# Decode step of two attention and two GLU layers: keeping one more V tile and passing the layer change through five single slots

## The chip, the cores and the metric

The kernel runs on one core of a Trainium2 chip. The metric is device time in microseconds of one execution, taken as the median of several executions. A core has a matrix engine (PE, with its weight loads shown apart as PEld), a vector engine (DVE), a scalar engine (ACT), a general engine (POOL) and a sync engine (SP). In this kernel SP issues all the large transfers from HBM into the on-chip memory (SBUF), in one fixed order; they run on 16 DMA engines that the core has. Sums of matrix products stand in PSUM, a memory of eight banks.

## What is computed

A residual block of attention and a residual block of a gated GLU, run twice with the same weights, for four sequences with one new token each:

```python
def _A_ref(x, k_cache, v_cache, wq, wo):        # x: 4 x 1 x 512
    W = min(4096, max(256, Sk // 4))            # 2048 of 8192 cached positions
    rep = Hq // Hkv                             # 32 query heads, 8 K/V heads
    q = (x @ wq)...                             # 4 x 32 x 1 x 128
    k = jnp.repeat(k_cache[:, :, Sk - W:, :], rep, axis=1)
    v = jnp.repeat(v_cache[:, :, Sk - W:, :], rep, axis=1)
    p = _softmax(q @ k.T * (Dh ** -0.5))
    return (p @ v)... @ wo

def _B_ref(x, w_gate, w_up, w_down):            # 512 -> 1792 -> 512
    return (_sigmoid(x @ w_gate) * (x @ w_up)) @ w_down

x = x + _A_ref(_layernorm(x), ...)
x = x + _B_ref(_layernorm(x), ...)
x = x + _A_ref(_layernorm(x), ...)
x = x + _B_ref(_layernorm(x), ...)
```

All weights and caches are bf16. The part of K that is read is 16 MB, that of V 16 MB, `wq` and `wo` are 4 MB each, the three GLU weights 1.8 MB each. Both attentions read the same caches and weights.

## The kernel before

**Memory.** One SBUF array, `arena`, is cut into 50 slots of 512 KB (128 partitions of 4096 bytes). Two neighbouring slots are a tile of 1 MB. Slots 0 to 31 hold all of K, loaded once and kept for both attentions. The other 18 slots are nine tiles of a pool (`pool`, line 372). Through these pass the V tiles (two per head, named `("V", h, bp, k)` with k = 0 or 1 for the first or second layer), `wq`, `wo` and the GLU weights. The four tiles of `wo` (two heads each) are loaded once in the first layer and kept to the end.

**Order of the loads.** A list `loads` (lines 1393 to 1420) fixes the order in which SP issues transfers. `fill` takes from its head as long as a place is free; the work that reads a place ends with `done`, which frees it. On the chip this becomes a wait of SP for the engine that last read the slot, and SP takes its queue strictly in order. In the first layer each head h brings K of head h + 2, every even head one tile of `wo` (`load_wo`), and then its two V tiles. After the last V come the GLU weights (`load_glu(0)`), `wq` for the second layer (`load_wq(1)`), the V tiles of the second layer from head 7 down, and the second GLU.

**What is kept over the layer change.** V of head 7 stays: tile Y = (7, 0) is moved into PSUM banks by four DVE transposes (`stash`, lines 564 to 570) and moved back later (`load_stash`, lines 572 to 581), so that its two slots are free meanwhile; tile Z = (7, 1) stays where it is, but its first half is also put into PSUM (`stash_half`, `unstash_half`), so that its first slot is free. V tile (6, 1) stays as a whole (`stay`, line 1396). The other 13 V tiles are read again.

**What passes through the change.** `homes` gives a load a fixed slot in place of one from the pool. Before the change there are seven such single slots: both of Y, the first of Z, and both of the tiles GA and GB, which first held the gate weights `wg` in two loads of 896 KB. Then follow, slot by slot, four loads of `wu`, four of `wd`, the second half of `wq` in four loads of 512 KB (`q_mms(1, 1, ...)` reads them), the first half of `wq` in two loads of 1 MB, and V tiles (6, 0) and (5, 1) in halves, in GA and GB.

**Order of the work.** In the first layer and the first GLU a planner (`_schedule`, line 92) picks the order on each engine from estimated durations and landing times; from `q_second` on (`P.chain`, line 1429) PE keeps the order of the program. `attn_first` (line 1146) runs, per head, four DVE transposes of K (line 830), scores (lines 848 and 859), a softmax (lines 872 to 887), a turn of the probabilities (lines 900 to 907), the product with V (`pv_unit`, line 949) and the product with `wo` (`wo_unit`, line 1137). `glu` (line 1268) runs eight groups of matmuls on `wg` and `wu` (line 1309) and four on `wd` (line 1377; in the last layer three, line 1352). `attn_second` (line 1167) begins with scores of head 7, between whose mask and products stand the first two groups of the first half of q (`q_mms(1, 0, OBS[1], (0, 1))`, line 1201; its matmuls are on line 769). Its V products for the first seven heads are `pv_wide` (line 1033); they use scratch in the place of a `wq` tile (`wide_buffers`, line 981). Only the last head goes through `pv_unit` and `wo_unit` again.

Of the kernel before, what the change touches and what calls it, by code (L numbers as in the profile page):

```python
# [278 lines left out]
def build(nc, A_x, A_k, A_v, A_wq, A_wo, B_wg, B_wu, B_wd, out, cfg=None):  # L279
# [42 lines left out]
    with es:  # L322
# [97 lines left out]
        GA = ("wg", 0, 0)  # L420
        GB = ("wg", 1, 0)
# [11 lines left out]
        def take_load():  # L433
            take_k()
            assert can_take()
            name, emit = loads.pop(0)
            if name in homes:
                hfree.difference_update(home(name))
                s = home(name)[0]
            else:  # L440
                s = pool.alloc()
            where[name] = s
            if name in (Y, Z, GA, GB):
                base[name] = s
            emit(s)
# [73 lines left out]
        def load_wq(k):  # L519
            if k == 0:  # L520
                for c in range(NC):
                    load(("wq", c, k), 2, "bw_8k", (2 * SLOT, wq_d[:, c, :], False))
            else:
                for c in range(NC):
                    load_half(("wq", c, k), wq_d[:, c, SLOT:2 * SLOT], "bw_4k", SLOT, ((Y, 1), (Z, 0), (GA, 0), (GA, 1))[c])
                for cc in range(NC // 2):
                    name = ("wq", (0, cc), k)
                    load(name, 2, "bw_4k", (2 * SLOT, wq_d[:, 2 * cc:2 * cc + 2, 0:SLOT], False))
                    homes[name] = [((GB, Y)[cc], 0), ((GB, Y)[cc], 1)]
                    if cc == 0:  # L530
                        on_free[name] = lambda s: hfree.add(s + 1)

        def wq_part(k, c, i):

            if k == 0:
                return ("wq", c, k), i * SLOT
            if i == 1:
                return ("wq", c, k), 0
            return ("wq", (i, c // 2), k), (c % 2) * SLOT

        def load_wo(hh):
            load(("wo", hh), 4, "bw_4k", (2 * SLOT, wo_d[:, hh * 2:(hh + 1) * 2, :], False))

        def load_glu(k):
            for nm, src in (("wg", wg_d), ("wu", wu_d)):
                if k == 0 and nm == "wu":
                    for c in range(NC):
                        load_half((nm, c, k), src[:, c, :], "bw_3k", F, ((Y, 0), (Y, 1), (Z, 0), (GA, 0))[c])
                    continue
                for cc in range(NC // 2):  # L550
                    load((nm, cc, k), 2, "bw_3k", (2 * F, src[:, 2 * cc:2 * cc + 2, :], False))
            on_free[GA] = lambda s: hfree.add(s + 1)
            on_free[GB] = lambda s: hfree.add(s + 1)
            for (a, b) in bounds_of(k):
                if k == 0:
                    load_half(("wd", a, k), wd_d[:, a:b, :].rearrange("p k n -> p (k n)"), "bw_4k", (b - a) * D,
                              ((GA, 1), (GB, 0), (GB, 1), (Y, 0))[a // 4])
                else:
                    load(("wd", a, k), 1, "bw_8k", ((b - a) * D, wd_d[:, a:b, :], False))
# [34 lines left out]
        def load_v(h, bp, k, n_use):  # L594
            name = ("V", h, bp, k)
            tile = {(HKV - 2, 0): GA, (HKV - 3, 1): GB}.get((h, bp)) if k else None
            if tile is not None:
                for n in range(2):
                    load_half((name, ("Vh", h, bp, k))[n], pair_d(A_v, h, bp)[:, :, n * SLOT:(n + 1) * SLOT], "bw_4k", SLOT, (tile, n))
                del on_free[name]  # L600
                halves[name] = ("Vh", h, bp, k)
                return
            load(name, n_use, "bw_8k", (2 * SLOT, pair_d(A_v, h, bp), True))
# [153 lines left out]
        def q_mms(k, i, qb, cs, keep_last=False):  # L757
            for c in cs:
                name, o = wq_part(k, c, i)
                s = need(name)  # L760

                half = k == 1 and i == 1
                src = slot_ap(s) if half else tile_ap(s)
                rd = tok(s) if k == 0 else tok(s)[:1] if half else tok(s)[c % 2:c % 2 + 1]

                def e_q(pe, c=c, src=src, o=o):
                    last = None
                    for hh in range(4):
                        last = pe.matmul(ps[32 * hh:32 * hh + NB, qb, :], xn[:, c * NB:(c + 1) * NB],  # L769
                                         src[:, o + hh * 512:o + (hh + 1) * 512],  # L770
                                         start=(c == 0), stop=(c == NC - 1))
                    return last
                P.op("tensor", "q%d_%d_%d" % (k, i, c), 4 * tm["pe_row"], e_q,
                     r=rd + [("xn",)], w=[("qrow", i)], banks=(qb,))
                if not (keep_last and c == NC - 1):
                    done(name)
                if k == 1 and i == 0 and c == 0:
                    give(s)
# [22 lines left out]
        def q_second(variance):  # L801
            q_mms(1, 1, WB, (0, 1))
            variance()
            unstash_half(())
            q_mms(1, 1, WB, (2, 3))
            fresh.append(q_turn(1, 1, WB))
# [174 lines left out]
        def wide_buffers(s, op):  # L981
            f = tile_ap(s).bitcast(F32)
            n = 0
            for name, size in (("tv", 512), ("o32", 32), ("osh", 32), ("rm", 64), ("rv", 8), ("pr", 8)):
                for k2 in range(2):
                    rest[name, k2] = f[:, n:n + size]
                    if name == "tv":
                        rest["dg", k2] = f[:, n:n + 544]
                    n += size
            for k2 in range(2):  # L990
                rest["A", k2] = f[:, n:n + 128].bitcast(BF16)
                n += 128
            rest["op"] = op
            rest["mb"] = f[:, n:n + 64]
            P.op("gpsimd", "mb", 200.0,
                 lambda g: g.tensor_copy(rest["mb"].rearrange("p (b x) -> p b x", b=2),
                                         maskb.unsqueeze(2).broadcast_to([128, 2, 32])),
                 r=[("maskb",)], w=[("mb",)], after=(op,))

        def sums(tag, k2):  # L1000
# [7 lines left out]
                 lambda pe: pe.matmul(out_, rest["mb"], pr, start=True, stop=True),  # L1008
                 r=[("pr", k2), ("mb",)], w=[("psb", k2)], banks=(sbank,))
# [8 lines left out]
        def pv_wide(tag, h, k2, tiles):  # L1018
            ob = OBS[k2]
            ew = ebuf[:, k2 * 256:(k2 + 1) * 256].bitcast(BF16).rearrange("p (g n x t) -> p g n t x", g=4, n=2, t=2)  # L1020
            ss = dict((bp, need(name)) for bp, name in tiles)
            for bp, name in tiles:
                if name in halves:
                    need(halves[name])

            def e_pv(pe):
                last = None
                for n in range(4):
                    mq, t = n // 2, n % 2
                    for g in range(4):  # L1030
                        jh, bp = g // 2, g % 2
                        src = tile_ap(ss[bp])[:, (jh * 16 + 8 * mq) * 128:(jh * 16 + 8 * mq + 8) * 128]
                        last = pe.matmul(ps[32 * g:32 * g + 32, ob, :], ew[:, g, mq, t],  # L1033
                                         src.rearrange("p (m t d) -> p t m d", t=2, d=128)[:, t], start=(n == 0), stop=(n == 3))
                return last
            P.op("tensor", "PV" + tag, 16 * tm["pe_row"], e_pv,
                 r=tok(ss[0]) + tok(ss[1]) + [("e", k2)], w=[("pso", k2, 0), ("pso", k2, 1)], banks=(ob,))
            for bp, name in tiles:
                done(name)
# [38 lines left out]
        def wo_wide(tag, h, op, k2, first, final):  # L1078
# [4 lines left out]
            def e_wo(pe):  # L1083
                last = None
                for m in range(REP):
# [4 lines left out]
                 r=tok(s) + [("opb", k2)], w=[("psr",)], banks=(PBS[1],))  # L1090
            done(name)

        def wo_compact(tag, h, op, k2):
# [4 lines left out]
            def e_wo(pe):  # L1098
                last = None
                for m in range(REP):  # L1100
# [6 lines left out]
                 r=tok(s) + [("opb", k2)], w=[("psw",)], banks=(WB,))  # L1107
# [20 lines left out]
        def wo_unit(tag, h, ov, k2, first, final):  # L1128
# [4 lines left out]
            def e_wo(pe):  # L1133
                last = None
                for r_ in range(REP):
# [7 lines left out]
                 r=tok(s) + [("op", k2)], w=[("psw",)], banks=(WB,))  # L1143
# [23 lines left out]
        def attn_second():  # L1167
# [33 lines left out]
            score(0, lambda: q_mms(1, 0, OBS[1], (0, 1)))  # L1201
# [4 lines left out]
            s = need(wq_part(1, NC - 1, 0)[0])  # L1206
            left[wq_part(1, NC - 1, 0)[0]] += 1
            q_mms(1, 0, OBS[1], (2, 3))
            wide_buffers(s, P.ops[-1])
# [58 lines left out]
        def glu(k, b0, b1, last=False):  # L1268
# [31 lines left out]
            for n, nm in enumerate(("wg", "wu")):  # L1300
                for c in range(NC):
                    piece = k == 0 and n == 1
                    name = (nm, c if piece else c // 2, k)
                    s = need(name) + (0 if piece else c % 2)
# [10 lines left out]
                    if k == 0 and n == 0 and c % 2 == 0:  # L1315
                        give(s)
# [79 lines left out]
        stay = keep[1:] + [(HKV - 2, 1)]  # L1396
# [3 lines left out]
        for h in range(HKV):  # L1400
            if h + 2 < HKV:
                loads.append((("K", h + 2), lambda _, h=h + 2: load_k(h)))
            if h % 2 == 0:
                load_wo(h // 2)
            for bp in range(2):
                load_v(h, bp, 0, 2 if (h, bp) in keep + stay else 1)
        load_glu(0)
# [3 lines left out]
        for h in range(HKV)[::-1]:  # L1411
            v_tiles[(0, h)] = [(bp, ("V", h, bp, 0)) for bp in range(2)]
            v_tiles[(2, h)] = [(bp, ("V", h, bp, 0 if (h, bp) in stay else 1)) for bp in range(2)[::-1]]
            for bp in range(2)[::-1]:
                if (h, bp) not in keep + stay:
                    load_v(h, bp, 1, 1)
                    n_v += 1
                    if n_v == cfg.get("ST", 2):
# [84 lines left out]
```

## Time and profile before

| What | Value |
|---|---|
| median of 3 runs | 180.72 us (180.55 to 181.25) |
| profiled execution, span | 178.8 us |
| busy: PE, DVE, ACT, POOL | 101.7, 104.4, 32.7, 21.5 us |
| bytes read from HBM | 70.78 MB |
| DMA, 20 to 80 us | 418 to 419 GB/s |
| DMA, 104 to 128 us (the layer change) | 358 to 417 GB/s in pieces of 4 us |
| first V product of head 7 in the first layer | 102.2 us |
| first GLU matmul | 108.46 us |
| first matmul of q for the second layer | 119.71 us |
| first softmax step of the second layer | 129.16 us |
| last matmul | ends at 176.15 us |

The page of the profile gives, per engine, the time in which it was busy, and then the span in 40 slices with the share of busy time in tenths. A row of a timeline gives the start, the time, the engine, the line of the kernel, the operation with its destination and source, the count of merged instructions and, in brackets, the idle time of that engine just before and what ended it. The instruction by which SP issues a transfer is line 398 (`SPq`); the transfer itself lands later. The trace also keeps, for each transfer, when each of the 16 DMA engines reported its part; the last of these reports is called its landing here.

### The profile page before, as it was taken

Reading aid. Unit: us, or ns where it says so; the run is one execution under the profiler, and the core shown is the slowest. Engines: PE = TensorE matmul, PEld = TensorE weight load, DVE = VectorE, ACT = ScalarE, POOL = GpSimd, SP = SyncE. Lnnn points to the kernel's source line nnn. Section 1 sums busy time; section 2 is a strip of 40 time slices with the busy share of each in tenths; the row PEclk is TensorE's granted clock in tenths of the full one; section 3 lists DMA queues with packets and bytes.
Section 4 is the critical chain, followed back from the end, with each engine's and each line's share of the span. In section 5 each row is a group of like instructions: output and inputs, shape, how many; then the busy total and the mean of one; then the engine's idle time right before and its main releaser. Section 6 shows DMA issues by size and latency. Waiting matters only on the chain.

```text
span 178.8 us, 3879 instructions
## 1 busy us (share of the span) xinstructions
PE 101.7 (57%) x1641; PEld 55.1 (31%) x1653; DVE 104.4 (58%) x256; ACT 32.7 (18%) x87; POOL 21.5 (12%) x87
## 2 busy tenths in 40 slices
PE   0635326481933626506436857455886999766743
PEld 0202101241521412403414743231322444435311
DVE  7308997838476384593564483324199999751431
ACT  2002031221030300301102001000143455430101
POOL 6100010101010100100101000000011543351000
PEclk9999999999999999999999999999999999975555
DMA  5999999999999999999999999999999999999980
GB/s 184 418 429 427 422 423 416 414 422 420 422 413 419 420 423 422 411 421 422 423 411 420 414 401 387 407 360 421 410 395 418 423 420 422 412 418 402 410 353 22
DMA packets 12802, 71.05 MB, mean 397 GB/s; under 512 B 1256, under 2 KB 1264, under 8 KB 6640
## 3 DMA queue, kind: packets, MB, share of 16 engines
q1 hardware_dynamic: 12776, 70.79, 96.9%
q8 instruction: 13, 0.21, 0.5%
q14 instruction: 5, 0.04, 0.1%
q10 hardware_dynamic: 8, 0.00, 0.0%
HBM read 70.78 MB, written 0.00 MB: 396 GB/s over the span
## 4 chain that ended last, share of the span: by engine, by line
DMA 35%; DVE 33%; PE 19%; SPq 4%; issue 4%; ACT 2%; POOL 1%; DVEq 0%; ACTq 0%
DMA arena<-in_A_v_cache_dram 20%; DVE arena L830 11%; DMA arena<-in_B_w_down_dram 9%; PE ps L859 7%; DVE nmax L872 5%; DMA arena<-in_A_wq_dram 5%; SPq L398 4%; PE ps L949 3%; DMA arena<-in_B_w_up_dram 2%; PE ps L848 2%; DVE arena L1041 2%; DVE nmax L876 2%; DVE ebuf L907 2%; DVE mxt L880 2%; PE ps L1137 1%
## 5 line engine op out<-in xcount | busy, mean ns | idle before, releaser
L830 DVE STREAM_TRANSPOSE arena<-arena 128x1024 f32<-128x1024 f32 x32 | 37.0, 1202 | 0.0
L859 PE MATMUL ps<-arena,qbd 128*32 128x512 bf16 x256 | 25.8, 539 | 0.0
L949 PE MATMUL ps<-ebuf,arena 128*128 128x8 bf16 x576 | 17.8, 168 | 9.2 <-DMA arena<-in_A_v_cache_dram 6.1
L872 DVE TENSOR_REDUCE nmax<-ps 128x1 f32<-128x512 f32 x16 | 10.8, 676 | 19.9 <-PE ps L859 19.8
L848 PE MATMUL ps<-msk_m,msk_s 128*32 128x512 bf16 x64 | 8.6, 526 | 23.0 <-DVE arena L830 21.8
L949 PEld LDWEIGHTS ps<-ebuf,arena 128*128 128x128 bf16 x576 | 16.8, 104 | 11.3 <-DMA arena<-in_A_v_cache_dram 7.3
L887 ACT ACTIVATE prow<-ps,nmax 128x512 bf16<-128x512 f32 x16 | 11.0, 687 | 35.1 <-DVE nmax L884 29.5
L823 ACT CAST qbd<-ps 128x256 bf16<-128x256 f32 x16 | 5.9, 370 | 45.4 <-PE ps L859 35.2
L916 POOL CAST s<-psm 128x1 bf16<-128x1 f32 x9 | 1.7, 188 | 84.1 <-ACT prow L887 84.1
L859 PEld LDWEIGHTS ps<-arena,qbd 128*32 128x32 bf16 x256 | 8.4, 122 | 10.6 <-issue 7.8
L902 ACT CAST prow<-ps 128x512 bf16<-128x512 f32 x16 | 9.4, 586 | 9.9 <-PE ps L949 2.1
L769 PE MATMUL ps<-arena,xn 128*4 128x512 bf16 x64 | 8.3, 575 | 5.0 <-DMA arena<-in_A_wq_dram 4.7
L907 DVE STREAM_TRANSPOSE ebuf<-prow 128x256 f32<-128x256 f32 x16 | 7.0, 435 | 3.8 <-ACT prow L902 3.7
L848 PEld LDWEIGHTS ps<-msk_m,msk_s 128*32 128x32 bf16 x64 | 1.7, 98 | 24.0 <-DVE arena L830 22.6
L1309 PE MATMUL ps<-arena,xn 128*4 128x448 bf16 x64 | 7.2, 559 | 3.4 <-DMA arena<-in_B_w_up_dram 2.3
L818 PE MATMUL ps<-qh,eyew 32*128 32x64 bf16 x64 | 5.6, 217 | 4.8 <-ACT qbd L823 2.4
L746 ACT ACTIVATE lnv<-ps 128x4 f32<-128x4 f32 x4 | 0.7, 174 | 41.5 <-PE ps L742 41.5
L1033 PE MATMUL ps<-arena,ebuf 128*32 128x512 bf16 x112 | 7.4, 384 | 0.2 <-DVE nmax L884 0.2
L957 DVE TENSOR_TENSOR onb<-ps,rinv 128x16 bf16<-128x16 f32 x9 | 1.7, 185 | 9.7 <-PE ps L949 9.7
L784 DVE STREAM_TRANSPOSE ebuf<-ps 128x512 f32<-128x512 f32 x3 | 2.2, 717 | 8.4 <-PE ps L769 8.2
L1137 PE MATMUL ps<-onp,arena 128*128 128x16 bf16 x144 | 5.3, 175 | 2.4 <-DVE onp L972 2.4
L818 PEld LDWEIGHTS ps<-qh,eyew 32*128 32x128 bf16 x64 | 3.3, 106 | 9.8 <-ACT qbd L823 5.4
(111 smaller groups left out, 131.1 us busy)
## 6 DMA issues: line engine op xcount, KB each, us to landing
arena<-in_A_v_cache_dram SPq DMA_DIRECT2D x27, 1024.0 KB, 21.4
arena<-in_A_k_cache_dram SPq DMA_DIRECT2D x16, 1024.0 KB, 25.1
arena<-in_A_wq_dram SPq DMA_DIRECT2D x6, 1024.0 KB, 8.4
arena<-in_A_wo_dram SPq DMA_DIRECT2D x4, 1024.0 KB, 24.7
arena<-in_B_w_gate_dram SPq DMA_DIRECT2D x4, 896.0 KB, 16.3
arena<-in_B_w_down_dram SPq DMA_DIRECT2D x4, 512.0 KB, 6.4
arena<-in_A_wq_dram SPq DMA_DIRECT2D x4, 512.0 KB, 8.2
arena<-in_A_v_cache_dram SPq DMA_DIRECT2D x4, 512.0 KB, 6.8
```

The lines of the kernel that those rows point to most:

```text
L769: last = pe.matmul(ps[32 * hh:32 * hh + NB, qb, :], xn[:, c * NB:(c + 1) * NB], src[:, o + hh * 512:o + (hh + 1) * 512], start=(c == 0), s ...
L818: last = pe.matmul(dst[:, :, a * REP:(a + 1) * REP], eyew[32 * hh:32 * hh + 32, 96 - 32 * a:224 - 32 * a], src, start=True, stop=True)
L830: P.op("vector", "T%d_%d" % (h, t), c_dve(1024), lambda v, v32=v32: v.transpose(v32, v32), r=[("slot", 4 * h + t)], w=[("slot", 4 * h + t)])
L848: last = pe.matmul(ps[32 * gi:32 * gi + 32, bank, :], msk_s[:, :], msk_m[:, :].unsqueeze(1).broadcast_to([128, 256, 2]), start=True, stop= ...
L859: last = pe.matmul(ps[32 * gi:32 * gi + 32, bank, :], qbd[:, q0:q0 + 32], kt[:, cp // 2, cp % 2, jh * NJ:(jh + 1) * NJ, :], start=False, s ...
L872: lambda v: v.tensor_reduce(nmax[:, k2:k2 + 1], ps[:, bank, :], AXX, ALU.max),
L887: lambda a: a.activation(prow[:, :].rearrange("p (m x t) -> p m x t", x=32, t=2), ps[:, bank, :].rearrange("p (m t x) -> p m x t", x=32, t ...
L902: P.op("scalar", "pc" + tag, c_act(512), lambda a: a.copy(prow[:, :], ps[:, pb, :]), r=[("ppb", pb)], w=[("prow",)], banks=(pb,))
L907: P.op("vector", "pt" + tag, c_dve(256), lambda v: v.transpose(et, prow[:, :].bitcast(F32)), r=[("prow",)], w=[("e", k2)])
L949: last = pe.matmul(ps[:, ob, bp * 8:bp * 8 + 8], src[:, j * 128:(j + 1) * 128], ev[:, j % 2, j % 16 // 2, x0:x0 + 8], start=(j == 0), stop ...
L1033: last = pe.matmul(ps[32 * g:32 * g + 32, ob, :], ew[:, g, mq, t], src.rearrange("p (m t d) -> p t m d", t=2, d=128)[:, t], start=(n == 0) ...
L1309: last = pe.matmul(ps[32 * g:32 * g + NB, gub[n], 0:NF], xn[:, c * NB:(c + 1) * NB], slot_ap(s)[:, g * NF:(g + 1) * NF], start=(c == 0), s ...
```

## The change

It does four things together.

- The last tile of `wo` (heads 6 and 7) leaves its place ahead of V of head 6 and is loaded behind the last V, as two transfers of 512 KB (`wo6`, `wo7`). Readers of `wo` now wait for the slot of their head alone.
- V tile (6, 0) joins `stay`, so that 12 V tiles are read again, not 13.
- GA is gone. GB becomes an empty pair of slots that is taken from the pool behind `wo7`. The layer change passes through five single slots: both of GB, both of Y, and the first of Z. `wg`, `wu`, `wd` of the first GLU and both halves of `wq` are all loaded slot by slot (448, 448, 512 and 512 KB, the last of `wd` 256 KB). V tile (5, 1) comes in two halves, into the second slot of GB and the first of Y.
- The first group of the first half of q moves from between mask and products of head 7 to `q_second`, in front of the transposes of the second half. The scratch of `wide_buffers` lies in two single slots, with a mask of its own in each. The stash of V (7, 0) comes back behind one V tile of the second layer, not two; in both kernels that is behind (5, 1).

```diff
-        GA = ("wg", 0, 0)
-        GB = ("wg", 1, 0)
+        GB = ("pair",)
...
-            if name in (Y, Z, GA, GB):
+            if name in (Y, Z, GB):
                 base[name] = s
+            if name == GB:
+                hfree.update((s, s + 1))
             emit(s)
...
-                for c in range(NC):
-                    load_half(("wq", c, k), wq_d[:, c, SLOT:2 * SLOT], "bw_4k", SLOT, ((Y, 1), (Z, 0), (GA, 0), (GA, 1))[c])
-                for cc in range(NC // 2):
-                    name = ("wq", (0, cc), k)
-                    load(name, 2, "bw_4k", (2 * SLOT, wq_d[:, 2 * cc:2 * cc + 2, 0:SLOT], False))
...
+                for i in (1, 0):
+                    for c in range(NC):
+                        load_half(("wq", c, k, i), wq_d[:, c, i * SLOT:(i + 1) * SLOT], "bw_4k", SLOT,
+                                  (((GB, 1), (Y, 0), (Y, 1), (GB, 0)), ((Y, 0), (Z, 0), (Y, 1), (GB, 0)))[i][c])
...
         def load_wo(hh):
-            load(("wo", hh), 4, "bw_4k", (2 * SLOT, wo_d[:, hh * 2:(hh + 1) * 2, :], False))
+            left["wo", hh] = 4
+
+            def emit(s):
+                for n in range(2):
+                    dma("wo%d" % (2 * hh + n), slot_ap(s + n), wo_d[:, 2 * hh + n, :], w=[("slot", s + n)], rate="bw_4k")
+
+            if 2 * hh + 2 < HKV:
+                load(("wo", hh), 4, "bw_4k", (2 * SLOT, wo_d[:, hh * 2:(hh + 1) * 2, :], False))
+            else:
+                loads.append((("wo", hh), emit))
...
             for nm, src in (("wg", wg_d), ("wu", wu_d)):
-                if k == 0 and nm == "wu":
+                if k == 0:
                     for c in range(NC):
-                        load_half((nm, c, k), src[:, c, :], "bw_3k", F, ((Y, 0), (Y, 1), (Z, 0), (GA, 0))[c])
+                        load_half((nm, c, k), src[:, c, :], "bw_3k", F,
+                                  (((GB, 0), (GB, 1), (Y, 0), (Y, 1)), ((Z, 0), (GB, 0), (GB, 1), (Y, 0)))[nm == "wu"][c])
...
                     load_half(("wd", a, k), wd_d[:, a:b, :].rearrange("p k n -> p (k n)"), "bw_4k", (b - a) * D,
-                              ((GA, 1), (GB, 0), (GB, 1), (Y, 0))[a // 4])
+                              ((Y, 1), (Z, 0), (GB, 0), (GB, 1))[a // 4])
...
-            tile = {(HKV - 2, 0): GA, (HKV - 3, 1): GB}.get((h, bp)) if k else None
...
+            tiles = {(HKV - 3, 1): ((GB, 1), (Y, 0))}.get((h, bp)) if k else None
...
             q_mms(1, 1, WB, (2, 3))
+            q_mms(1, 0, OBS[1], (0,))
             fresh.append(q_turn(1, 1, WB))
...
-            score(0, lambda: q_mms(1, 0, OBS[1], (0, 1)))
+            score(0, lambda: q_mms(1, 0, OBS[1], (1,)))
...
-            s = need(wq_part(1, NC - 1, 0)[0])
-            left[wq_part(1, NC - 1, 0)[0]] += 1
+            slots = []
+            for c in (NC - 2, NC - 1):
+                name = wq_part(1, c, 0)[0]
+                slots.append(need(name))
+                left[name] += 1
             q_mms(1, 0, OBS[1], (2, 3))
-            wide_buffers(s, P.ops[-1])
+            wide_buffers(slots, P.ops[-1])
...
-        stay = keep[1:] + [(HKV - 2, 1)]
+        stay = keep[1:] + [(HKV - 2, 1), (HKV - 2, 0)]
...
-            if h % 2 == 0:
+            if h % 2 == 0 and h + 2 < HKV:
                 load_wo(h // 2)
             for bp in range(2):
                 load_v(h, bp, 0, 2 if (h, bp) in keep + stay else 1)
+        load_wo(HKV // 2 - 1)
+        loads.append((GB, lambda s: None))
         load_glu(0)
         load_wq(1)
...
-                    if n_v == cfg.get("ST", 2):
+                    if n_v == cfg.get("ST", 1):
                         load_stash(("V",) + keep[0] + (1,))
```

What is left out of the diff carries the same through: `pv_wide` takes its V from four slots in place of two tiles, `glu` takes each group of weights from a slot of its own, and the readers of `wo` name one slot.

## The prediction

> **What bounds the kernel now.** I read the page first, for the load on the engines and the DMA.
>
> ```profile
> PE 101.7 (57%) x1641; PEld 55.1 (31%) x1653; DVE 104.4 (58%) x256; ACT 32.7 (18%) x87; POOL 21.5 (12%) x87
> ...
> DMA  5999999999999999999999999999999999999980
> GB/s 184 418 429 427 422 423 416 414 422 420 422 413 419 420 423 422 411 421 422 423 411 420 414 401 387 407 360 421 410 395 418 423 420 422 412 418 402 410 353 22
> ...
> q1 hardware_dynamic: 12776, 70.79, 96.9%
> ```
>
> No engine is busy for much over half of the span, and the DMA engines always are, at some 420 GB/s, except in slices 24 to 30 (103 to 134 us), the layer change. So bytes set the time, as long as transfers are issued early enough. Next, therefore, the transfers of the layer change (issues in the window 92 to 135 us: count, size, median us from issue to landing) and the line of SP's issues in 90 to 135 us.
>
> ```profile
> arena<-in_A_wq_dram SPq DMA_DIRECT2D x4, 512.0 KB, 8.2
> ...
> arena<-in_A_v_cache_dram SPq DMA_DIRECT2D x4, 512.0 KB, 6.8
> ...
> arena<-in_B_w_up_dram SPq DMA_DIRECT2D x4, 448.0 KB, 5.9
> arena<-in_B_w_down_dram SPq DMA_DIRECT2D x3, 512.0 KB, 6.0
> ```
>
> ```profile
> DMA to landing us min/median/max: 4.3/7.2/10.4
> ```
>
> I call the time from issue to landing the lead. It shows how much work the DMA engines still had in front of a transfer. The shortest lead is 4.31 us (`wu` c = 3, issued at 109.04, landed at 113.35), and it landed 1.11 us behind its forerunner, the plain time of its 0.459 MB. So 4.3 us is still enough.
>
> Last, the timeline where the second attention ends (start, time, engine, line; in brackets what ended the idle time before).
>
> ```profile
> 159.92 1.01 PE L949 MATMUL ps<-ebuf,arena 128*128 128x8 bf16 x32 [0.41 <-DMA arena<-in_A_v_cache_dram]
> ...
> 161.84 0.21 PE L1067 MATMUL ps<-msks,arena 64*128 64x8 bf16 x2 [0.47 <-POOL arena L1053]
> 162.32 0.59 PE L1102 MATMUL ps<-opb,arena 128*128 128x4 bf16 x16 [0.27 <-ACT opb L1073]
> 162.77 0.99 PE L949 MATMUL ps<-ebuf,arena 128*128 128x8 bf16 x32
> ```
>
> ```profile
> 171.38 0.92 PE L1309 MATMUL ps<-arena,xn 128*4 128x448 bf16 x8 [1.30 <-DMA arena<-in_B_w_up_dram]
> ...
> 173.89 1.02 PE L1352 MATMUL ps<-arena,hT 128*4 128x128 bf16 x32 [1.17 <-DMA arena<-in_B_w_down_dram]
> 175.11 1.01 PE L1352 MATMUL ps<-arena,hT 128*4 128x128 bf16 x24 [0.20 <-DMA arena<-in_B_w_down_dram]
> ```
>
> The last V product (162.77) follows a chain of POOL, ACT and PE, not its V, which landed at 162.37. Only from 171.38 on does PE wait for weights again. So from the first softmax step (129.16) to about 170 the second attention runs at its own pace, and the DMA sets the end by the last `wu` and `wd` alone.
>
> **What goes.** One V tile is 1.049 MB; at 420 GB/s (slices 2 to 23) that is 2.5 us of DMA. It lies behind the layer change, so every landing after (5, 1) comes 2.5 us earlier if the DMA never runs dry: the last `wu` at 168.85 and not 171.34, the three `wd` at 171.35, 172.55 and 173.2 and not 173.85, 175.07 and 175.69. The bytes up to the end of `wq` are the same as before, so those landings keep their places.
>
> **What the end can take of it.** With the attention unmoved, the mean and variance end at 169.11 and PE goes through: `wu` c = 0 to 3 from 169.17 to 171.0 (two rows of 0.92), transpose 171.05 to 171.70, product 171.74 to 171.96 (0.65 and 0.22, as at 172.35 and 173.04), first `wd` at 172.10 (0.36 from the start of the product to it, as at 114.67 and 115.03), then 1.02, 0.60 and 0.41: 174.1, against 176.15 now. That is a gain of 2.05. If the attention starts at least 0.45 earlier, the `wd` landings bind again and the gain is 2.5.
>
> **The start of the second attention.** Now two groups of q (row at 126.33, 1.07 for both) stand between mask and scores of head 7; the second becomes the only one. The first goes to PE behind the group that ends at 124.34, when its 512 KB have landed (the old pair landed at 126.27, so the first half at about 125.0): 125.05 to 125.65, and the spread of q (line 818, now 125.63) follows with no loss. Scores come one group earlier, by 0.45 to 0.5. The four DVE transposes that bring Y back (0.62 each, 130.67 to 133.14) keep their place behind the first softmax.
>
> **wo behind the last V.** V of heads 6 and 7 lands one place earlier: (6, 0) 94.49, (6, 1) 96.98, (7, 0) 99.47, (7, 1) 101.95, then `wo6` 103.2, `wo7` 104.44. The V product of head 6 is bound by the turn of its softmax (98.95 to 100.8), as now. Head 7 follows at 101.4 and 102.4 in place of 102.20 and 104.48. `wo` of head 6 waits until 103.25, of head 7 until 104.6 (oe, pm, oq as now: 1.1 us behind V), against 106.39. First GLU matmul: 106.7, against 108.46. But the last `wg` lands at 108.90 as before, so GLU meets the same landings, and the 1.8 us buy only earlier issues. PE's queue behind the waiting `wo` holds nothing but head 7 and the layer norm. The stash (four of 0.68) moves from 101.97 to 99.5; it can hold up one small DVE step by 0.68, under the wait for `wo6`.
>
> **The five slots.** For each load I take the end of the last reader from the rows of its kind (0.55 us for a group of `wg` or `wu`, 0.60 for q, 0.57 for `wd`), and as landing the same place in the byte order now.
>
> | load, slot | freed by | issue | lands | lead |
> |---|---|---|---|---|
> | wg 2, 3 (Y) | V of head 7, stash | 102.5, 102.9 | 107.78, 108.90 | 5.3, 6.0 |
> | wu 0 (Z) | half stash behind oq, 0.73 | 105.3 | 110.02 | 4.7 |
> | wu 1, 2 (GB) | wg 0, 1 | 107.3, 107.85 | 111.14, 112.24 | 3.8, 4.4 |
> | wu 3, wd 0 (Y) | wg 2, 3 | 108.45, 109.55 | 113.35, 114.63 | 4.9, 5.1 |
> | wd 1 (Z) | wu 0 | 111.0 | 115.91 | 4.9 |
> | wd 2, 3 (GB) | wu 1, 2 | 111.8, 112.9 | 117.19, 117.87 | 5.4, 5.0 |
> | q2 0 (Y) | wu 3 | 114.0 | 119.10 | 5.1 |
> | q2 1 (Z) | wd 1 | 116.6 | 121.16 | 4.6 |
> | q2 2, 3 | SP's queue; wd 2 | 117.0, 117.85 | 122.43, 123.71 | 5.4, 5.9 |
> | q1 0, 1 | wd 3, q2 0 | 118.3, 120.35 | 125.0, 126.27 | 6.7, 5.9 |
> | q1 2, 3 | q2 2, 3 | 123.1, 124.4 | 127.55, 128.82 | 4.4, 4.4 |
> | V (5, 1) | q1 0, 1 | 125.7, 127.0 | 130.10, 131.34 | 4.4, 4.3 |
> | V (5, 0) | scores of head 7 | 128.7 | 133.85 | 5.1 |
>
> The leads fall from a median of 7.2 to about 5, and one, 3.8, lies under the shortest seen. A needed lead below 4.3 is bounded from the start of the kernel: the first transfer, 1 MB on empty queues, was issued at 0.79 and landed at 5.77, so 2.5 us besides its bytes; with 1.1 for 448 KB that is 3.6. From above, the median of `wu`, 5.9, may be what is needed. I take 3.6 to 4.3, because a row at 4.31 shows no loss: a cost of 0 to 0.5. At 5.9 the worst place (3.8) is 2.1 late; and a slot's round of lead and 0.7 for its reader, 6.6, is longer than five places of 1.25, 6.25, by 0.35 in each of four rounds: 3.5 in all.
>
> **Small parts.** Three more issues on SP (`wo` 1, `wg` 2, `wq` 2, V two fewer) at 0.33 to 0.53 each hide in SP's waits (27.6 us for the V products alone). The second mask is one more POOL step of 0.24, before a sum that PE reads 0.98 us after it (133.16 plus 0.32, read at 134.47). The scratch and the slot-wise waits cost nothing of their own. Were these covers gone: 1.6 and 0.24.
>
> **A rule against it.** Halves of 512 KB of `wq` land 1.27 to 1.28 us apart, the 1 MB tiles of `wq` 2.55, so a split costs no rate here while transfers queue up. The Trainium skill (DMA: Bandwidth & Descriptors, Bandwidth and Rules for kernel authors) asks for at least 1 MiB per DMA, and its section on the anatomy of a DMA fits 2.0 us of fixed cost to each, on another issuing path than SP's. Were that paid openly by each of the three added transfers, the sum would be 184.4 in place of 178.4; by the row it is 178.4.
>
> **Sum and forecast.** 2.05 with no earlier start, 2.5 with 0.45 earlier; 0 to 0.5 for late slots. I take 2.3. Span 178.8 - 2.3 = 176.5; the median stands 1.9 above the profiled span, so 180.72 - 2.3 = **178.4**. Its own range is 177.7 to 179.2: at the low end also the gap before `q2 1` (2.06 in place of 1.28 us, with the packets slow but the DMA busy) goes.
>
> **Rivals.** *PE takes wo first.* The planner might put `wo` of head 6 ahead of head 7's V. For it speaks that it comes first in the program; against it that V (7, 0) is there 3.7 us before `wo6`. Then PE waits until 103.2, Y is free at 104.9 (103.2 + 0.6 + 1.0), the lead of wg 2 is 2.9, and it lands 0.7 to 1.4 late (3.6 and 4.3 needed), with everything behind it. Gain 2.3 - 1.05 = 1.25: 179.5, between 179.1 and 179.9.
>
> *The five slots run dry.* With a needed lead of 5.9 the loss is 3.5 and the gain 2.5 or less: 180.72 + 1.0 = 181.7. The place is `wu 1` to V (5, 1), the point from which it turns slower is a needed lead of 5.65, where 1.85 at the worst place and 0.1 in each of four rounds make 2.3. For it: from 128.8 to 131.3 us the DMA moves 360 GB/s at a share of 0.96, although the leads there are 6 to 7. Against it: the row at 4.31.
>
> *The second attention hides the saving.* If its start does not move and the clock granted to PE, 0.50 from about 159 on, spreads forward, the gain shrinks to 1 to 1.5: 179.2 to 179.7. The matmuls of line 1309 take 0.56 at both clocks, so I give it little.
>
> **Chances.** Forecast 0.68; wo first or hidden saving 0.18; slots run dry 0.14. The measurement can tell about 0.5%, 0.9 us, from no change. Faster (under 179.8): 0.66 + 0.11 = 0.77. Slower (over 181.6): most of the last, 0.11. Within: 0.12. Range 177.7 to 180.3: the forecast, the middle cases and the mild end of dry slots.
>
> **What would show it.** V in 27 transfers of 1 MB and two halves, 69.7 MB read. Leads of 4 to 6 in the layer change and slices there still at 9 in DMA; last V product of head 7 near 103.4, first GLU matmul near 106.7; first softmax step of the second layer near 128.7; PE at the end going from `wu` 1 to `wu` 2 without a wait. It would be wrong if that softmax step came after 130, or if a row of the layer change waited over 1 us for weights issued under 5 us before.

## The result, and the profile after

The changed kernel takes 183.43 us in the median (181.57 to 184.37, six runs); the kernel before took 180.99 beside it (180.49 to 181.45, six runs). The ratio is 1.0108 [1.007, 1.0145]: slower by 1.1%. The ratio leaves out the run of 184.37, which lies over 1.5% above the fastest of its kernel and counts as slow; the medians alone would give 1.0135. 178.4 was predicted, with a range that ended at 180.3. The span of the profiled execution grew from 178.8 to 181.7, at the same granted clock (0.945).

Again the page first: load on the engines, then the DMA share and GB/s in 40 slices, then the queue of the large transfers.

```profile
PE 101.9 (56%) x1641; PEld 54.9 (30%) x1653; DVE 104.1 (57%) x256; ACT 32.7 (18%) x87; POOL 21.6 (12%) x88
...
DMA  5999999999999999999999999989989999999990
GB/s 196 417 427 429 424 417 422 408 426 415 417 420 422 422 415 418 418 424 424 415 420 423 402 341 321 376 312 343 347 229 416 424 427 418 418 416 403 410 372 18
...
q1 hardware_dynamic: 12568, 69.74, 95.5%
```

The engines do what they did before, and the tile is gone from the bytes (70.79 to 69.74 MB). Nearly all that differs lies in slices 24 to 30, the layer change: 229 to 376 GB/s, where before 360 to 421 stood. Pieces of 4 us over the same stretch (columns: busy time and count of PE, PEld, DVE, ACT, POOL; granted clock; DMA share; GB/s), after:

```profile
104.00:108.00 4.00, 1.96 (x30) 1.48 (x34) 2.65 (x10) 0.00 (x0) 0.00 (x0) 1.00 0.95 354
108.00:112.00 4.00, 2.35 (x22) 0.71 (x10) 1.58 (x4) 0.72 (x4) 0.00 (x0) 1.00 0.87 309
...
120.00:124.00 4.00, 1.58 (x14) 0.71 (x11) 0.96 (x6) 0.00 (x0) 0.00 (x0) 1.00 0.89 312
124.00:128.00 4.00, 2.01 (x14) 0.68 (x10) 2.41 (x4) 0.38 (x2) 0.00 (x0) 1.00 0.96 326
...
132.00:136.00 4.00, 3.43 (x36) 1.01 (x35) 3.87 (x10) 2.01 (x5) 0.23 (x2) 1.00 0.80 212
```

and before:

```profile
108.00:112.00 4.00, 3.20 (x27) 1.08 (x27) 1.79 (x8) 0.72 (x4) 0.00 (x0) 1.00 1.02 382
...
120.00:124.00 4.00, 2.26 (x18) 0.77 (x14) 1.50 (x3) 0.38 (x2) 0.00 (x0) 1.00 1.02 416
...
132.00:136.00 4.00, 3.04 (x48) 1.30 (x51) 3.73 (x11) 1.20 (x3) 0.82 (x3) 1.00 1.05 428
```

After the change the DMA share falls under 0.9 in three places: some of the 16 DMA engines had nothing to do. Counted in pieces of 0.5 us, the mean number of DMA packets under way is lowest at 109.5 (10.0), 119.5 (11.9) and 132.5 us (9.9). The line of SP's issues in 90 to 137 us (minimum, median, maximum of the lead; before in 90 to 135: 4.3, 7.2, 10.4):

```profile
DMA to landing us min/median/max: 3.7/6.1/9.7
```

So the leads did not fall to about 5 in the median. For the 21 loads of the prediction's table alone the median is 5.6, where the table has 5.0: a lead also grows when the transfer itself comes late. What waits for them, in the timeline (start, time, engine, line; in brackets the idle time before and what ended it):

```profile
103.05 0.59 PE L1137 MATMUL ps<-onp,arena 128*128 128x16 bf16 x16 [0.26 <-DMA arena<-in_A_wo_dram]
...
103.87 0.73 DVE L588 STREAM_TRANSPOSE ps<-arena 128x512 f32<-128x512 f32 x1
...
104.51 0.18 DVE L958 TENSOR_TENSOR onb<-ps,rinv 128x16 bf16<-128x16 f32 x1
...
107.48 1.81 PE L1311 MATMUL ps<-arena,xn 128*4 128x448 bf16 x16 [0.36 <-DVE xT L734]
...
112.72 0.54 PE L1311 MATMUL ps<-arena,xn 128*4 128x448 bf16 x4 [2.04 <-DMA arena<-in_B_w_up_dram]
...
116.54 0.57 PE L1377 MATMUL ps<-hT,arena 128*128 128x4 bf16 x16 [1.10 <-DMA arena<-in_B_w_down_dram]
...
117.82 0.59 PE L1377 MATMUL ps<-hT,arena 128*128 128x4 bf16 x16 [0.72 <-DMA arena<-in_B_w_down_dram]
...
123.70 0.59 PE L772 MATMUL ps<-arena,xn 128*4 128x512 bf16 x4 [1.58 <-DMA arena<-in_A_wq_dram]
...
128.34 0.59 PE L772 MATMUL ps<-arena,xn 128*4 128x512 bf16 x4 [1.58 <-DMA arena<-in_A_wq_dram]
...
131.99 0.69 DVE L873 TENSOR_REDUCE nmax<-ps 128x1 f32<-128x512 f32 x1 [4.10 <-PE ps L860]
...
174.27 0.92 PE L1311 MATMUL ps<-arena,xn 128*4 128x448 bf16 x8 [1.32 <-DMA arena<-in_B_w_up_dram]
```

The wait at 112.72 is for `wu 1`, that at 123.70 for `q2 1`. The first softmax step of the second layer comes at 131.99, not 128.7 (before: 129.16), and the end is later by about as much: the last `wu` lands at 174.22 in place of 171.34, although a whole tile less stands before it.

### The profile page after: what moved, and what is told of

It is laid out like the page before. It is cut to its first block, busy times and chain, and to the rows that moved or that the text cites. A ratio compares the mean times of both kernels' runs of the same rounds, so it can differ in the third digit from the quotient of the medians.

```text
span 181.7 us, 3884 instructions
## 1 busy us (share of the span) xinstructions
PE 101.9 (56%) x1641; PEld 54.9 (30%) x1653; DVE 104.1 (57%) x256; ACT 32.7 (18%) x87; POOL 21.6 (12%) x88
## 3 DMA queue, kind: packets, MB, share of 16 engines
q1 hardware_dynamic: 12568, 69.74, 95.5%
## 4 chain that ended last, share of the span: by engine, by line
DMA 34%; DVE 34%; PE 20%; issue 4%; SPq 3%; ACT 3%; POOL 1%; DVEq 0%; ACTq 0%
DMA arena<-in_A_v_cache_dram 15%; DMA arena<-in_B_w_down_dram 12%; DVE arena L831 11%; PE ps L860 7%; DVE nmax L873 5%; DMA arena<-in_A_wq_dram 4%; PE ps L950 4%; SPq L398 3%; DMA arena<-in_B_w_up_dram 3%; PE ps L849 2%; DVE arena L1041 2%; DVE ebuf L908 2%; DVE nmax L877 2%; DVE mxt L881 2%; PE ps L1137 1%
## 5 line engine op out<-in xcount | busy, mean ns | idle before, releaser
L1320 DVE STREAM_TRANSPOSE ebuf<-ps 128x448 f32<-128x448 f32 x4 | 2.6, 650 | 8.4 <-PE ps L1311 8.4
```

## Where the time went

To reckon it I take, for each transfer, how much later than its forerunner it landed, less the plain time of its bytes at 411 GB/s, the rate of weights and halves (whole V tiles come at 421, so their losses are put 0.06 too low). I call this its **loss**. Beside it stands the work that was still **queued** ahead when SP issued it: landing of the forerunner minus issue. For the places where the changed kernel lost most:

| load | issued | forerunner landed | queued | landed | loss |
|---|---|---|---|---|---|
| `wu 1` | 108.07 | 109.78 | 1.72 | 112.68 | 1.78 |
| `q2 1` | 118.44 | 120.92 | 2.48 | 123.65 | 1.46 |
| V (5, 1), first half | 128.98 | 132.02 | 3.03 | 134.57 | 1.28 |
| V (5, 1), second half | 130.28 | 134.57 | 4.29 | 137.09 | 1.24 |

Transfers that were issued between 90 and 133 us lost 1.65 in all before (0.79, 0.42 and 0.66 at `wq` second half c = 1 and two V loads, with 6.2, 4.3 and 5.2 us queued, and next to nothing at the others) and 6.62 after. The change thus gave back 4.97 and saved 2.5 (the tile): 2.5 slower by this account, and the span says 2.9. The slots are not only few: `q2 1` takes Z, which the second `wd` group frees (117.82 and 0.59 above), and stands in SP's queue ahead of `q2 2`, whose slot the first `wd` group had freed 1.3 earlier (116.54 and 0.57). No run has the five slots in another order, so "the five slots" means below: in this order.

The experiments ask whether the five slots did it (**theory A**: SP may issue only when a slot is free, and with five that is too late), or the loads being smaller (**theory B**), or `wo` behind the last V (**theory C**).

## The experiments

Each kernel has a ratio to the kernel before, which ran beside it (medians 181.33, 180.88 and 181.24 in the three batches). In five kernels one to four slots of the kept K of head 0 are used as extra slots. This overwrites them, so that the second attention of that head multiplies by weights; the work stays the same.

**Seven and six slots.** The changed kernel with two or one more slots in the rotation (the diff is that for seven; for six `range(2)` is `range(1)`, and the lists of slots follow suit).

```diff
-        base = {}
+        X = ("K", 0)
+        base = {X: 0}
+        hfree.update(range(2))
...
-                                  (((GB, 0), (GB, 1), (Y, 0), (Y, 1)), ((Z, 0), (GB, 0), (GB, 1), (Y, 0)))[nm == "wu"][c])
+                                  (((GB, 0), (GB, 1), (X, 0), (X, 1)), ((Y, 0), (Y, 1), (Z, 0), (GB, 0)))[nm == "wu"][c])
...
```

> The changed kernel with seven single slots in the layer change in place of five; the two more are the first two slots of K of head 0, so K of head 0 is overwritten and the second attention of that head is computed from weights. Theory A (five slots are too few: a transfer is issued too late to begin when the DMA engines run out of work): the DMA of the layer change is full again as in the kernel before, the saved V tile shows, 177.5 to 179.5 us. Rival B (the many transfers of 448 and 512 KB are themselves slow): 182.5 to 184, as the changed kernel. Rival C (wo behind the last V delays the first layer's end and with it the change): 182.5 to 184.

> The same with six single slots (one slot of K of head 0 more than the changed kernel has, its contents overwritten). Theory A: between five and seven, 179.5 to 181.5 us. Rivals B and C: 182.5 to 184, no difference from five slots.

179.62 with seven, ratio 0.9898 [0.9865, 0.9932]; 179.93 with six, 0.9933 [0.9903, 0.9963]. With the very same bytes, order and transfer sizes, one slot more turns 1.1% slower into 0.7% faster. Pieces of 4 us with seven slots:

```profile
108.00:112.00 4.00, 2.86 (x22) 0.80 (x14) 1.59 (x4) 0.72 (x4) 0.00 (x0) 1.00 1.03 406
...
120.00:124.00 4.00, 2.62 (x18) 0.77 (x14) 1.84 (x4) 0.38 (x2) 0.00 (x0) 1.00 1.02 388
124.00:128.00 4.00, 3.56 (x33) 1.10 (x33) 0.64 (x2) 0.37 (x1) 0.00 (x0) 1.00 1.03 410
128.00:132.00 4.00, 3.51 (x40) 1.14 (x37) 3.75 (x9) 2.01 (x5) 0.15 (x1) 1.00 0.91 337
132.00:136.00 4.00, 2.82 (x42) 1.14 (x43) 3.66 (x13) 1.15 (x3) 0.84 (x4) 1.00 1.01 385
```

The stretches that stood at 309 to 326 GB/s are full; only 128 to 132 still dips, where V (5, 0) is late (2.96 queued, 1.52 lost). PE waits 1.7 us for `wq`, as before the change, in place of 3.8. The Trainium skill (Perfetto Trace Analysis, Optimization Strategy) says that the same gap, repeating over a stretch on the engine that should be saturated, can mean that SBUF has no room for the next tile. Here the gaps are of unequal size, but they go when slots are added: the three pieces with a DMA share of 0.80 to 0.89 stand at 1.01 to 1.03 with seven slots.

**wo alone, small loads alone.** The kernel before, with only the last `wo` tile moved behind the last V; and the kernel before with `wg` and the first half of `wq` in loads of 448 and 512 KB into the same slots.

```diff
-            if h % 2 == 0:
+            if h % 2 == 0 and h + 2 < HKV:
                 load_wo(h // 2)
...
+        load_wo(HKV // 2 - 1)
```

```diff
+                if (name[0] == "wg" and name[2] == 0) or (name[0] == "wq" and name[2] == 1):
+                    for n in range(2):
+                        dma(str(name), dst[:, n, :], src[:, n, :], w=[("slot", s + n)], rate=rate)
+                    return
```

> The kernel before with only the last tile of wo moved behind the last V, as two transfers, and the readers of wo waiting for one slot. Theory A: no change, 180.5 to 181.5 us. Rival C: most of the loss, 182.5 to 184. Rival B: 181 to 181.5.

> The kernel before with only the loads of wg and of the first half of wq in the layer change cut into single slots (448 and 512 KB each), same places, same order. Theory A: no change, 180.5 to 181.5 us. Rival B: slower by 1.5 to 3, 182.5 to 184. Rival C: no change.

`wo` moved: 180.65, 0.9963 [0.9939, 0.9987]. Loads split: 181.23, 0.9987 [0.9953, 1.002]. Neither costs anything that can be measured, so theories B and C fall. The six and seven slots say the same: they have the small loads and the late `wo` too. The Trainium skill (DMA: Bandwidth & Descriptors, Rules for kernel authors) asks for 1 MiB or more per DMA; this run shows no price for 448 and 512 KB, with at least 3.25 us queued ahead of each. Of the kernels that compute all that the reference does, the first of the two has the lowest ratio, though by less than the noise.

**Where the slot is missing.** The sixth slot only for `wg`, `wu`, `wd` (a narrower theory: the early place `wu 1` does it all), and only from `wq` on.

```diff
-                                  (((GB, 0), (GB, 1), (Y, 0), (Y, 1)), ((Z, 0), (GB, 0), (GB, 1), (Y, 0)))[nm == "wu"][c])
+                                  (((GB, 0), (GB, 1), (X, 0), (Y, 0)), ((Y, 1), (Z, 0), (GB, 0), (GB, 1)))[nm == "wu"][c])
...
-                              ((Y, 1), (Z, 0), (GB, 0), (GB, 1))[a // 4])
+                              ((X, 0), (Y, 0), (Z, 0), (Y, 1))[a // 4])
```

```diff
-                                  (((GB, 1), (Y, 0), (Y, 1), (GB, 0)), ((Y, 0), (Z, 0), (Y, 1), (GB, 0)))[i][c])
+                                  (((GB, 1), (X, 0), (Y, 0), (Y, 1)), ((X, 0), (Y, 0), (Y, 1), (GB, 0)))[i][c])
```

> The changed kernel with a sixth slot (one of K of head 0, its contents overwritten) for wg, wu and wd only; from wq on five slots. Theory A1 (the DMA engines mostly run dry in the GLU, 106 to 111 us): near the six-slot run, 180 to 181 us. Theory A2 (mostly at wq and the first V, 119 to 136 us): near the changed kernel, 182 to 183.5. Rival D (no single place; every round of the five slots loses a little): about halfway, 181 to 182.

> The reverse: five slots for wg, wu and wd, the sixth (a slot of K of head 0, overwritten) from wq on, in the place that Z's first slot has for the second part of wq. Theory A2: 180 to 181 us. Theory A1: 182 to 183.5. Rival D: 181 to 182.

Early only: 183.96, 1.015 [1.0075, 1.0224]. Late only: 182.51, 1.0072 [1.0028, 1.0116]. The early slot does free `wu 1` (2.97 queued, no loss), but then a load of `wq` is issued at 117.79 with 1.22 queued and loses 1.31, and all losses add up to 7.0, as in the changed kernel (6.6). The time is longer than any theory had put it (183.5 at most), and here too the order of the slots has a part: the load issued at 117.79 takes Z, freed by the third `wd` group, while GB's second slot, freed by the last `wu` group, goes to the load behind it. So `wu 1` is not the one bad place; that any order of these slots would lose as much is not shown.

**Five slots, nothing saved.** The changed kernel with V (6, 0) read again.

```diff
-        stay = keep[1:] + [(HKV - 2, 1), (HKV - 2, 0)]
+        stay = keep[1:] + [(HKV - 2, 1)]
...
-                    if n_v == cfg.get("ST", 1):
+                    if n_v == cfg.get("ST", 2):
```

> The changed kernel with V (6, 0) read again as before: five slots, but no saved tile (2.5 us more to read). Theory A: the five slots lose as much as in the changed kernel, so 184 to 186 us; somewhat less if the tile, which needs none of the five slots, covers the last gap at the first V. Rival E (keeping the tile is what hurts, through the pool): 180.5 to 181.5, as the kernel before.

185.64, 1.0239 [1.0173, 1.0304]. The tile itself is worth 185.64 - 183.43 = 2.2 us (by the ratios, 1.0239 - 1.0108 = 1.3%, 2.4 us). The saving was there, and the slots took more.

**Half stash out of the way.** The changed kernel with the first half stash behind the step that scales head 7's output (`oe`, line 958), not ahead of it.

```diff
-                    stash_half(0, "st3")
                 op = pv_unit(tag, h, h % 2, v_tiles[(0, h)])
+                if h == HKV - 1:
+                    stash_half(0, "oe" + tag)
```

> The changed kernel, all of it computed, with the first half stash of Z (a DVE transpose of 0.73 us) put behind the scaling of the last head's output in place of ahead of it. Theory A: the end of the first layer and with it three issues come some 0.5 to 0.9 us earlier, so 182.4 to 183.2 us against 183.4. Rival D or A2: no change that can be measured.

183.61, 1.0128 [1.0038, 1.0218], where theory A had 182.4 to 183.2. The first GLU matmul comes at 106.95 in place of 107.48, near the 106.7 of the prediction, and no gain is seen, in a wide interval: `wu 1` is issued 0.5 earlier, still has only 2.47 queued, and loses 1.30.

**Lateness alone, with all slots in place.** In the runs so far a slot's number and the time of the issue changed together. These three leave the kernel before as it is, and only hold back the issue of one load, `wq` second half c = 1, by one more wait: for the last `wu` group (as in the diff), the second `wd` group (`gd0_4`), or the third (`gd0_8`).

```diff
+        by_name = dict((o.name, o) for o in P.ops)
+        by_name[str(("wq", 1, 1))].deps.add(by_name["glwu0_3"])
```

> The kernel before, its six slots and its order untouched; only the second half of `wq` of the column half c=1 waits, beside its slot, for the matmuls of the last `wu` group, which are over at about 114.0 us in the trace of before. Its transfer's forerunner lands at about 119.1 there, so some 5 us of work are still queued at the issue: the control for the two kernels with the same wait put later. By the theory that a load loses nothing as long as about 3.5 us of work are queued ahead of it: no change, 180.5 to 181.5. By the rival that any wait which is added here costs time: 0.5 us or more longer.

> The same with the wait put on the second `wd` group, about 116.6 us: the load is issued with some 2.5 us of work still queued ahead of it. By the theory that under 3.5 us of queued work the transfer engines run dry: it lands 0.5 to 1.6 us later than its 1.28 us behind its forerunner, and all behind it with it: 181.3 to 182.5. By the rival that what the change lost came from reuse of the slots and not from how late the loads are issued: no change, 180.5 to 181.5, since every slot here is free as early as before.

> The same with the wait put on the third `wd` group, about 117.9 us: some 1.2 us of work are queued ahead at the issue. By the theory: 1.3 to 2.5 us later behind its forerunner than the plain time, so 182 to 183.5, and longer than the kernel with the wait on the second group. By the rival: no change, 180.5 to 181.5.

| wait for | issued | queued | its loss | us | ratio |
|---|---|---|---|---|---|
| last `wu` | 113.80 | 5.14 | 0.56 | 180.98 | 0.9978 [0.9952, 1.0005] |
| second `wd` | 116.49 | 2.52 | 1.40 | 182.45 | 1.0072 [1.0048, 1.0095] |
| third `wd` | 117.73 | 1.20 | 1.53 | 183.72 | 1.0153 [1.0106, 1.02] |

Without any wait, in the kernel before, this load was issued at 112.87 with 6.23 queued and lost 0.79; so the later waits add 0.6 and 0.7 to its own loss, not 1.4 and 1.5.

Pieces of 4 us, with the wait for the last `wu`, and then for the third `wd`:

```profile
116.00:120.00 4.00, 2.39 (x45) 1.72 (x42) 0.96 (x6) 0.00 (x0) 0.00 (x0) 1.00 1.01 356
120.00:124.00 4.00, 2.39 (x18) 0.77 (x14) 1.43 (x2) 0.38 (x2) 0.00 (x0) 1.00 1.03 413
```

```profile
116.00:120.00 4.00, 2.39 (x46) 1.74 (x43) 0.96 (x6) 0.00 (x0) 0.00 (x0) 1.00 0.75 259
120.00:124.00 4.00, 1.88 (x14) 0.68 (x10) 1.43 (x2) 0.38 (x2) 0.00 (x0) 1.00 0.98 358
```

With 5 us queued an added wait costs nothing that can be measured. With 1.2 queued, a quarter of the DMA's time in that piece is gone (0.75), and one load held back, with the three that stand behind it in SP's queue, makes the kernel 1.5% slower: about as much as the whole change. No slot is missing here, so it is the late issue that costs. But most of the price, 2.8, is not the load's own: two loads behind it, with 4.3 and 5.7 queued, lost 0.59 and 1.74, which the queued time does not explain.

**Nine slots.** Four slots of K of head 0 added.

```diff
+        X = ("K", 0)
+        base = {X: 0}
+        hfree.update(range(4))
```

> The changed kernel with nine slots: four slots of the kept K of head 0 are added to the five and are overwritten, so head 0 of the second attention computes its scores from weights. By the theory that the gain of slots ends where 3.5 us are always queued: as with seven slots, 179 to 180 (that kernel had 2.4 us left, 2.2 of it at the V tile that needs the first tile of K of the second attention, which no slot helps). By the rival that more slots always give more: below 178.5.

177.88, 0.9812 [0.9787, 0.9837]. Below 178.5: here the rival was right, the gain had not ended at seven. The end then waits for bytes alone:

```profile
170.99 1.02 PE L1354 MATMUL ps<-arena,hT 128*4 128x128 bf16 x32 [1.15 <-DMA arena<-in_B_w_down_dram]
172.23 1.01 PE L1354 MATMUL ps<-arena,hT 128*4 128x128 bf16 x24 [0.21 <-DMA arena<-in_B_w_down_dram]
```

Part of the step from seven to nine lies outside of the layer change. With seven slots, one V tile lost 1.0 at 156 us (its 16 parts landed from 153.06 to 156.03, against some 1.9 us of spread in the tile ahead), though it had been issued 18 us before; with nine this is not seen. What makes it is open.

**All runs in one account.** Columns: loads issued in 90 to 133 us with under 3.5 us queued; what all loads issued there lost; the span that follows from it (178.8, plus that loss less the 1.65 of before, less 2.5 where the tile is saved); the span measured; the ratio.

| kernel | under 3.5 | lost | span reckoned | span | ratio |
|---|---|---|---|---|---|
| before | 1 of 24 | 1.65 | | 178.8 | 1 |
| after, five slots | 4 of 25 | 6.62 | 181.3 | 181.7 | 1.0108 |
| seven slots | 1 of 27 | 1.92 | 176.6 | 177.5 | 0.9898 |
| six slots | 2 of 27 | 2.43 | 177.1 | 177.5 | 0.9933 |
| `wo` late | 0 of 25 | 2.05 | 179.2 | 179.7 | 0.9963 |
| split | 1 of 28 | 2.73 | 179.9 | 180.3 | 0.9987 |
| six, early only | 3 of 25 | 7.03 | 181.7 | 182.0 | 1.015 |
| six, late only | 3 of 27 | 4.76 | 179.4 | 179.7 | 1.0072 |
| five, 13 tiles | 4 of 26 | 6.18 | 183.3 | 184.3 | 1.0239 |
| five, half stash later | 4 of 25 | 6.85 | 181.5 | 182.8 | 1.0128 |
| wait for `wu` | 1 of 24 | 2.77 | 179.9 | 179.7 | 0.9978 |
| wait for second `wd` | 2 of 22 | 3.15 | 180.3 | 180.4 | 1.0072 |
| wait for third `wd` | 2 of 22 | 4.09 | 181.2 | 180.9 | 1.0153 |
| nine slots | 1 of 27 | 1.35 | 176.0 | 175.9 | 0.9812 |

The span follows from the losses to within 0.5 us in ten of the thirteen kernels that differ from before; with seven slots, 13 tiles and the later half stash it is 0.9 to 1.3 longer. In these three, V tiles issued after 133 us with 5 to 15 us queued lost 1.0, 1.3 and 1.4 more (single tiles up to 1.0), which fills the difference in size; what delayed them is open.

## Why the prediction was wrong, point by point

**The tile saved: right.** 2.5 us were predicted; five slots with and without the tile differ by 2.2 to 2.4, and with nine slots the time is 1.88% below before (3.4 us; 2.9 by the spans of the profiled executions), no less than the forecast of 2.3.

**wo and the end of the first layer: right in what mattered.** The matmul of `wo` for head 6 at 103.05 (predicted 103.25). For head 7 the half stash (103.87, 0.73) stood ahead of the output step and delayed it, against the prediction, whose table has a half stash behind `oq` alone; the GLU began at 107.48, not 106.7. Taking it away changed nothing that can be seen in the time.

**Small loads and more issues: right.** The split run gives 0.9987; the rule's sum of 184.4 lies near the time measured, but for another reason.

**The five slots: the step that failed.** "I take 3.6 to 4.3, because a row at 4.31 shows no loss: a cost of 0 to 0.5", said the prediction of the needed lead. The cost was 4.97. Three things were wrong in it.

First, the lead is the wrong measure: it includes the transfer's own time and every gap in the DMA. `q2 1` had a safe-looking lead of 4.6 in the table, but its forerunner was to land at 119.10, 2.5 after its issue at 116.6; the rest of the lead was the gap of 2.06 that before already showed there. In the run the shortest lead of all, 3.67 (`wu 0`), lost nothing, while `wu 1`, with 4.61, lost 1.78.

Second, one row that lost nothing stood for the rule. That row (`wu` c = 3 of before) had 3.19 us queued. Over all 14 profiled kernels, the loads issued in 90 to 133 us:

| queued at issue, us | loads | lost over 0.5 us | mean loss, us | of `wq` and V | of the others |
|---|---|---|---|---|---|
| under 2.5 | 8 | 8 | 1.56 | 4 of 4 | 4 of 4 |
| 2.5 to 3.5 | 21 | 10 | 0.63 | 9 of 10 | 1 of 11 |
| 3.5 to 5 | 94 | 10 | 0.13 | 10 of 42 | 0 of 52 |
| 5 to 6 | 86 | 11 | 0.14 | 11 of 47 | 0 of 39 |
| over 6 | 145 | 3 | 0.03 | 3 of 75 | 0 of 70 |

The last two columns count the losses over 0.5 us apart, for `wq` and V and for `wo`, `wg`, `wu` and `wd`. At 2.5 to 3.5 nearly every load of `wq` and V loses and nearly no `wu` does (the others there are all `wu`). So one limit does not hold for all, and the row of before, a `wu`, stood in the prediction for `wq` and V too. The 354 loads are the same few places in 14 kernels, not as many independent cases.

Third, each landing was kept at its place. `q2 1` was to be issued at 116.6 and was issued at 118.44, because `wd 1`, whose slot it takes, landed at 117.77 in place of 115.91; its queued work, 2.48, stayed as small as in the table, since its forerunner was late too. `wu 1` was worse off than in the table (1.72 queued, not 2.7), because the GLU began 0.8 later.

The prediction's own table, read by what is queued, has eight places under 3.5: `wu 1` 2.7, `wu 2` 3.3, `q2 1` 2.5, `q1 2` and `q1 3` 3.2 each, V (5, 1) 3.1 and 3.1, V (5, 0) 2.6. At the mean loss of 0.63, which only these runs gave, eight lose 5.0, and 180.72 - 2.3 + 5.0 = 183.4. That it meets the median of 183.43 is partly luck: of the eight, `wu 1`, `q2 1` and the two halves of V (5, 1) lost, and 0.91 more was lost by `q1 0`, with 5.99 queued. The ratio puts the kernel at 180.72 x 1.0108 = 182.7.

Both signs of being wrong that the prediction named came: the first softmax step after 130 (131.99), and a wait of over 1 us for weights issued under 5 us before (2.04 for `wu 1`, issued 4.61 before it landed).

**The rivals.** *The five slots run dry* was the case that came, at 181.7 with a chance of 0.14. The 360 GB/s in 128.8 to 131.3 that spoke for it was set aside on the row at 4.31; the loads there had 4.3 us and more queued, so it is no plain sign of dry slots either. Its price, 3.5, was 1.5 too low, and its picture of one worst place (2.1) and 0.35 in each round did not come: five loads lost 0.9 to 1.8 each. *PE takes wo first* did not happen. *The second attention hides the saving* did not either: with nine slots the saving reaches the end.

**What stays open.** What sets `wq` and V, which lose with up to 6.2 us queued, apart from `wu` and the other loads; how much of the cost goes with the order of the slots and not with their number; why loads that are issued in a burst behind a late one lose more with over 4 us queued; and what delayed single V tiles behind the layer change, as with seven slots.

## What to carry to other kernels

Where transfers set the time and go through few recycled slots, look at each load's issue against the landing of its *forerunner*, not against its own landing: here under 2.5 us of queued work was a loss in every case, and at 2.5 to 3.5 in nine of ten for `wq` and V, in one of eleven for `wu`. Don't carry a row of one kind of load over to another. A tile kept on the chip saves its bytes only if the slots that it takes don't push issues under that mark: one slot (512 KB) decided here between 1.1% slower and 0.7% faster. Before trusting a threshold, hold back one load of the kernel as it is by a wait and see what it costs.

## What was not expected of the hardware

A transfer behind work that is running out can take longer to land than one on empty queues. The first transfer of the kernel took 2.5 us besides its bytes. In the eight cases with under 2.5 us queued, the queued time and the loss together, which is the same measure (the lead less the bytes), came to 2.5 to 4.3 us (1.22 and 1.31 at the lowest, 2.49 and 1.80 at the highest). So the bound of 3.6 us that the prediction drew from the cold start was too low. The parts of one transfer don't land together either, even where nothing is lost: the four `wu` of before took 1.4 to 1.9 us from the first part to the last, where their 448 KB take 1.12; `wu 1` after took 2.1 (110.56 to 112.68).

Little of a loss is made up later: the DMA engines move 413 to 428 GB/s in most slices of both kernels, so nearly all of what the loads lose stands at the end, 40 to 60 us on: the last `wu` is 2.9 later, and 4.97 lost less 2.5 saved is 2.5.
